# A recurrence and an MLP in float32: the first MLP product as three one-pass products of 12-bit parts

## The chip, the cores and the metric

The kernel runs on one core of a Trainium2 chip. The metric is the device time of one execution in microseconds (us). A core has a matrix engine (PE, TensorE), three engines for elementwise work (DVE or VectorE, ACT or ScalarE, POOL or GpSimd), an engine that only issues transfers here (SP), and DMA queues. Each engine works through its own instructions in the order in which the program placed them, and waits for others by semaphores. PE writes its results to PSUM, a small memory in banks; DVE and ACT bring them from there to SBUF, the main working memory.

## The reference

Two blocks stand one behind the other. The first is a linear recurrence for each of 4 x 8 pairs of batch and head, with 768 steps of 48 channels:

```python
for t in range(S):
    cur = einsum('bhd,bhe->bhde', u[None] * k_t, v_t)
    y[:, :, t] = einsum('bhd,bhde->bhe', r_t, state + cur)
    state = w_t[:, :, :, None] * state + einsum('bhd,bhe->bhde', k_t, v_t)
```

Its output, with the heads side by side, is x of 4 x 768 x 384. The second is a normalization and an MLP with 1536 hidden columns:

```python
xn = (x - mu) / sqrt(var + 1e-6) * g_ln
out = x + maximum(xn @ w_ch1, 0.0) @ w_ch2
```

All of it is float32.

## The kernel before

There are 8 rounds, each half of a batch's steps (384) for all heads; a round has two units of four heads. In a round the recurrence is solved by six levels of doubling blocks. At each level PE makes block products of r and k (`quads`, tile `a_ps`), DVE multiplies r and k by decays (`grow`), and DVE copies the wanted blocks into A with a mask (`keep`):

```python
def grow(q, lev, which="rk"):          # one unit
    ...
    for nm in which:
        ...
        DVE.tensor_tensor(out=X, in0=X, in1=T[...].broadcast_to(blocks), op=ALU.mult)

def keep(rnd, lev):
    for j in range(2):
        ...
        DVE.copy_predicated(out=out_j[:, :, :, 1, :], mask=mask, data=ps_j)
```

After the levels, the next round's first levels carry the states (`states`: PE makes `kv`, DVE a chain of small multiply-adds `s`) and the outputs (`outputs`: PE makes `y`, DVE adds it to `vo`). Inputs come with time on the partitions and are turned by PE with an identity matrix, three 128x128 pieces into one PSUM tile that ACT copies out (`turned` for w, k and r, `ends` for `kn`, `turned_x` for the normalized x):

```python
ps_t = ctx.enter_context(tc.tile_pool(name="ps_t", bufs=2, space=PSUM))
ps_a = ctx.enter_context(tc.tile_pool(name="ps_a", bufs=2, space=PSUM))
ps_m = ctx.enter_context(tc.tile_pool(name="ps_m", bufs=2, space=PSUM))
```

The MLP of a round is a generator of 24 steps. Twelve steps make one h tile each, and twelve steps make three o products each (in round 0 two of the o tiles run together):

```python
def mlp(rnd):
    ...
    for f in range(FC):                # FC = 12
        converted(KC * (f * P // WC + 1))
        ps = ps_m.tile([P, RN], F32, tag="m", name=f"h_ps{name}_{f}")
        for kc in range(KC):           # KC = 3
            PE.matmul(ps, w1_sb[:, kc, ts(f, P)], xT[:, kc, :], start=kc == 0, stop=kc == KC - 1)
        hs.append(ph.tile([P, RN], F32, tag="h", name=f"h{name}_{f}"))
        ACT.activation(out=hs[f], in_=ps, func=AF.Relu)
        yield
    # then: for each of three row tiles, 12 products with w2_sb into o_ps,
    #       DVE adds x into a tile o, SP sends o out
```

The main loop goes through rounds and levels. Each slot of round and level issues `quads`, `grow` and `keep`, and then `fill(UNTIL[slot], tasks)` lays a list of other tasks (transposes, loads, copies) evenly between MLP steps until a given number of steps is done. A round's MLP starts late in the next round's levels; from round 3 on a slot holds four steps, so that the h tiles of one round's MLP fall into level 5 and levels 0 and 1, and its o products into levels 2 to 4. During rounds 0 and 1 the weights are also brought into a rounded form by ACT and DVE (`begin`, `join`). `warm` issues matmuls whose results nobody reads.

Of the kernel before, what the change touches and what calls it, by code (L numbers as in the profile page):

```python
# [9 lines left out]
F32 = mybir.dt.float32  # L10
F16 = mybir.dt.float16
I8 = mybir.dt.int8
# [5 lines left out]
PSUM = bass.MemoryType.PSUM  # L18

# [25 lines left out]
def kernel(  # L53
# [45 lines left out]
    p6 = ctx.enter_context(tc.tile_pool(name="p6", bufs=6))  # L99
    low = ctx.enter_context(tc.tile_pool(name="low", bufs=4))  # L100
    ph = ctx.enter_context(tc.tile_pool(name="ph", bufs=12))
    ps_t = ctx.enter_context(tc.tile_pool(name="ps_t", bufs=2, space=PSUM))
    ps_a = ctx.enter_context(tc.tile_pool(name="ps_a", bufs=2, space=PSUM))
    ps_m = ctx.enter_context(tc.tile_pool(name="ps_m", bufs=2, space=PSUM))
# [8 lines left out]
        for nm in "wkr"  # L113
    }
    vn, vx, xs = {}, {}, {}
# [6 lines left out]
    def load(q, which="wkr", eng=SP):  # L122
        for nm in which:
            src = {"w": w, "k": k, "r": r}[nm]
            for j in range(NH):
                eng.dma_start(
                    out=nat[nm][q % 2][:, ts(j // 2, TT), j % 2, 0:D], in_=steps(src, q, j)
                )

    def load_v(q, eng=SP):  # L130
        vn[q] = p4.tile([P, NH, TT, D], F32, tag="v", name=f"v{q}")
        for j in range(NH):
            eng.dma_start(out=vn[q][:, j], in_=steps(v, q, j))

    def load_vx(q, eng=SP):

        vx[q] = p4.tile([P, NP, TT, D], F32, tag="vx", name=f"vx{q}")
        for i in range(2):
            eng.dma_start(
                out=vx[q][ds(C * (1 - i), C)].rearrange("p r c d -> p r (c d)"),  # L140
                in_=vn[q][ds(C * i, C)]
                .rearrange("p (r j) c d -> p r j (c d)", j=2)[:, :, 1],
            )
# [25 lines left out]
    for nm in "wkr":  # L169
        for t in nat[nm]:  # L170
            POOL.memset(t[:, :, :, D:HP], 0.0)
# [8 lines left out]
    for lev in range(NLEV - 1):  # L180
# [21 lines left out]
    w1_sb = const.tile([P, KC, DF], F32, name="w1_sb")  # L202
# [3 lines left out]
        (w1_sb[:, kc, ds(c, WC)], moe_w_ch1[ts(kc, P), ds(c, WC)])  # L206
# [59 lines left out]

    def warm(n):

        ps = ps_m.tile([P, RN], F32, tag="m", name="idle")
        for _ in range(n):  # L270
            PE.matmul(ps[:, 0:P], zeros, zeros, start=True, stop=True)


    st, carry = {}, {}

    def turned(q, nm, pr):
        a = st.setdefault(q, {})
        if pr == 0:
            if nm == "w":
                if q % U == 0:  # L280
                    st["w"] = p1.tile([P, U, W], F32, tag="w", name=f"wT{q // U}")
                a["w"] = st["w"][:, q % U]
            else:
                a[nm] = p4.tile([P, W], F32, tag=nm, name=f"{nm}T{q}")
        ps = ps_t.tile([P, RN], F32, tag="t", name=f"{nm}_ps{q}_{pr}")
        for c in range(TT):
            PE.transpose(
                ps[:, ts(c, P)],
                nat[nm][q % 2][:, pr * TT + c].rearrange("p j d -> p (j d)"), ident,
            )  # L290
        ACT.copy(out=a[nm][:, ts(pr, RN)], in_=ps)

    def totals(rnd, eng):

        tot = p1.tile([P, U, W], F32, tag="tot", name=f"tot{rnd}")
        T = [st["w"]]
        at, n = 0, W // 2
        for lev in range(NLEV):
            pair = T[lev].rearrange("p u (q two) -> p u q two", two=2)
            if lev < NLEV - 1:  # L300
                t = tot[:, :, at : at + n]
            else:
                t = p3.tile([P, U, NM], F32, tag="decay", name=f"decay{rnd}")
            eng.tensor_tensor(out=t, in0=pair[..., 0], in1=pair[..., 1], op=ALU.mult)
            T.append(t)
            at, n = at + n, n // 2
        for q in units_of(rnd):
            st[q]["T"] = [t[:, q % U] for t in T]


    def own_products(q, eng):
        b, f, g = units[q]
        rk = st[q]["rk"] = p1.tile([P, NK, 2, D], F32, tag="rk", name=f"rk{q}")
        eng.tensor_tensor(
            out=rk, in0=nat["k"][q % 2][:, :, :, 0:D], in1=nat["r"][q % 2][:, :, :, 0:D],
            op=ALU.mult,
        )
        by_tile = rk.rearrange("p (r c) j d -> p r c (j d)", r=NP)
        eng.tensor_tensor(
            out=by_tile, in0=by_tile,  # L320
            in1=u_bc[:, ts(g, NH)].rearrange("p (r j) d -> p r (j d)", j=2)[:, :, None]
            .broadcast_to([P, NP, TT, 2 * D]), op=ALU.mult,
        )
# [9 lines left out]
    def own_by_pe(q):  # L333
        b, f, g = units[q]
        a = st[q]
        ps = ps_t.tile([P, RN], F32, tag="t", name=f"own_ps{q}")
# [16 lines left out]
    def own_term(q, eng):  # L353
        a = st[q]
        a["vo"] = p4.tile([P, NH, TT, D], F32, tag="vo", name=f"vo{q}")
        eng.tensor_tensor(
            out=a["vo"], in0=vn[q],
            in1=a["own"][:, :, :, None].broadcast_to([P, NH, TT, D]), op=ALU.mult,
        )
# [23 lines left out]
    def grow(q, lev, which="rk"):  # L383

        n = 1 << lev
        a = st[q]
        T = (a["T"][lev] if lev else a["w"]).rearrange("p (q two) -> p q two", two=2)
        blocks = [P, W // (2 * n), n]
        for nm in which:
            i = "kr".index(nm)  # L390
            X = a[nm].rearrange("p (q two n) -> p q two n", two=2, n=n)[:, :, i, :]
            DVE.tensor_tensor(
                out=X, in0=X, in1=T[:, :, 1 - i][:, :, None].broadcast_to(blocks), op=ALU.mult
            )
# [3 lines left out]
    def keep(rnd, lev):  # L398
        n = 1 << lev
        A, ps = a_bufs[rnd % 2], a_ps[rnd]  # L400
        for j in range(2):
# [6 lines left out]
            else:  # L408
                mask = masks[lev][:, None].broadcast_to([P, U * NK, C // (2 * n), n])
                DVE.copy_predicated(out=out_j[:, :, :, 1, :], mask=mask, data=ps_j)  # L410
# [15 lines left out]
    def ends(q, pr):  # L426

        a = st[q]
        if pr == 0:
            a["kn"] = p2.tile([P, NK, P], F32, tag="kn", name=f"kn{q}")  # L430
        ps = ps_t.tile([P, TT, P], F32, tag="t", name=f"kn_ps{q}_{pr}")
# [4 lines left out]
    def states(q):  # L436
# [3 lines left out]
        s = a["s"] = p4.tile([P, NP, 2 * TT, D], F32, tag="s", name=f"s{q}")  # L440
        before = carry.get((b, g))
        kv = ps_a.tile([P, 2, 512], F32, tag="a", name=f"kv{q}")
# [9 lines left out]
        for m in range(2 * TT - (f == NHALF - 1)):  # L452
            for pr in range(NP):
                new = kv[:, m % 2, pr * TT + m // 2, :]
                if m == 0 and before is None:
                    DVE.tensor_copy(out=s[:, pr, m, :], in_=new)
                else:
                    c = pr * 2 * TT + m
                    DVE.scalar_tensor_tensor(
                        out=s[:, pr, m, :], in0=s[:, pr, m - 1, :] if m else before[:, pr, 2 * TT - 1, :],  # L460
# [3 lines left out]
        carry[b, g] = s  # L464
# [11 lines left out]
    def outputs(q):  # L476
# [7 lines left out]
        for k_ in range(NK):  # L484
# [9 lines left out]
            for i in range(2):  # L494
                for j in range(2):
# [5 lines left out]
                    elif a["before"] is not None:  # L501
                        R, s = a["r"][rows, ts(2 * k_, C)], a["before"][rows, pr, 2 * TT - 1]
# [44 lines left out]
    def turned_x(rnd, kc):  # L547
        if kc == 0:
            xTs[rnd] = p1.tile([P, KC, RN], F32, tag="xT", name=f"xT{rnd}")
        ps = ps_t.tile([P, RN], F32, tag="t", name=f"xT_ps{rnd}_{kc}")  # L550
        for i in range(TT):
# [3 lines left out]
        ACT.activation(  # L555
            out=xTs[rnd][:, kc, :], in_=ps, func=AF.Copy, scale=g_sb[:, kc : kc + 1]
        )

    def mlp(rnd):
# [3 lines left out]
        for f in range(FC):  # L563
            converted(KC * (f * P // WC + 1))
            ps = ps_m.tile([P, RN], F32, tag="m", name=f"h_ps{name}_{f}")
            for kc in range(KC):
                PE.matmul(
                    ps, w1_sb[:, kc, ts(f, P)], xT[:, kc, :], start=kc == 0, stop=kc == KC - 1
# [3 lines left out]
            yield  # L572

        groups = ((0, 1), (2,)) if rnd == 0 else ((0,), (1,), (2,))
        at = 0
        for group in groups:
# [13 lines left out]
            for i in group:  # L590
                o = p2.tile([P, H, D], F32, tag="o", name=f"o{name}_{i}")
                DVE.tensor_tensor(out=o, in0=ps[i], in1=x[:, i], op=ALU.add)
                SP.dma_start(
                    out=out[b, ds(f0 * RN + i * P, P), :].rearrange("t (h d) -> t h d", d=D),
                    in_=o,
# [58 lines left out]
    grow(u0, 0)  # L654
# [10 lines left out]
    grow(u1, 0)  # L665
# [3 lines left out]
    for lev in range(1, NLEV):  # L669
# [9 lines left out]
        for which in ("rk",) if lev < NLEV - 1 else "kr":  # L679
            for q in (u0, u1):  # L680
                grow(q, lev, which)
# [31 lines left out]
    mlps.append(mlp(0))  # L713

# [8 lines left out]
    for rnd in range(1, NR + 1):  # L723
# [3 lines left out]
        for lev in range(NLEV):  # L727
# [11 lines left out]
            for which in ("rk",) if lev < NLEV - 1 else "kr":  # L739
                for q in now:  # L740
                    grow(q, lev, which)
            if now:
                if rnd <= 2 and lev == 0:
                    totals(rnd, DVE)
                keep(rnd, lev)
            tasks = []
            if rnd == 1:
                if lev < 2:
                    tasks += each(load, new, "kr"[lev], [SPO])
# [14 lines left out]
            if rnd == 2 and lev == 0:  # L764
                tasks += each(load_v, now) + each(load, new, "w")
            if rnd == 2 and lev == 2:
                for q in now:
                    take(DVE, q)
                    tasks += each(load, new[q % U :][:1], "kr")
            if rnd == 2 and lev in (3, 4):  # L770
                tasks += each(own_term, now[lev - 3 :][:1], [POOL])
            if rnd > 2 and lev < 2:
                tasks += each(load, new, ["w", "kr"][lev])
# [13 lines left out]
            if lev == 3 and rnd > 1:  # L787
                for q in now:
                    load_vx(q)
                for q in new:  # L790
                    load_v(q)
# [6 lines left out]
            if lev == 5:  # L798
                if rnd > 2 and new:
                    own_sums(new[0])  # L800
                if rnd == 2:
                    tasks += each(own_products, new[:1], [POOL]) + each(own_sums, new[:1])
                if rnd >= 2:
                    tasks += each(own_term, new[:1], [POOL])
# [4 lines left out]
                if rnd >= 2:  # L809
                    tasks += each(own_sums, new[1:]) + each(own_term, new[1:], [POOL])  # L810
# [37 lines left out]
```

## Time and profile before

| | before |
|---|---|
| time, median of 3 runs | 620.29 us (620.15 to 621.03) |
| span of the profiled execution | 624.0 us |
| PE busy | 588.7 us, 8588 matmul records |
| DVE, ACT, POOL busy | 294.2, 199.2, 70.2 us |
| DMA moved | 36.83 MB |
| matmul groups `o_ps`, `h_ps`, `a_ps` | 205.5, 198.4, 82.1 us |

Busy time counts an interval once where instructions of an engine overlap; a mean duration counts each instruction with its overlap. Matmuls are pipelined, so that the spacing of their starts, and not their duration, is their rate. "PEld" are the loads of PE's stationary operand. In a group's row, the part after the last bar is the idle time of the engine just before these instructions, with what ended it. The chain is the sequence of work and waits that leads back from the last instruction to the first. Tile names carry the program's names without numbers; all instructions of the kernel have one line, that of the helper which keeps program order.

### The profile page before, as it was taken

To read this page: it belongs to the slowest core of one execution; us is meant where nothing else is said; L and a number is where in the kernel's file an instruction comes from. 1 tells how busy PE (TensorE), PEld (TensorE's weight loads), DVE (VectorE), ACT (ScalarE), POOL (GpSimd) and SP (SyncE) were. 2 spreads that over 40 slices of the span, in tenths; PEclk is the share of its full clock that TensorE was granted. 3 is DMA by queue.
4 is the path that set the end of the run, shared out by engine and by line. 5 is a ranking of instruction groups with operands and counts; after the bars stand their busy time and mean duration, and the time that the engine had idled before them with its cause. 6 is when DMAs were issued, how large, how long until landed. Compare 5 with 4: busy or idle time off the path is not lost.

```text
span 624.0 us, 19313 instructions
## 1 busy us (share of the span) xinstructions
PE 588.7 (94%) x8588; PEld 401.3 (64%) x8588; DVE 294.2 (47%) x706; ACT 199.2 (32%) x430; POOL 70.2 (11%) x100
## 2 busy tenths in 40 slices
PE   8969887987999999999999999999999999999997
PEld 7859554555666676667666676676666766566554
DVE  3854986785544755444437253553336352130000
ACT  3535675540135321431143212531142105301200
POOL 5000000000216100700051002500050000000000
PEclk9786898986699999999999999998999999999999
DMA  7872788103343241223220430211000000000000
GB/s 113 186 174 67 176 212 209 47 3 84 65 85 59 39 95 44 40 41 76 48 52 12 78 75 15 39 22 43 23 15 2 15 15 15 0 15 25 1 13 26
DMA packets 114962, 36.83 MB, mean 59 GB/s; under 512 B 104512, under 2 KB 111808, under 8 KB 114880
## 3 DMA queue, kind: packets, MB, share of 16 engines
q1 hardware_dynamic: 112464, 35.31, 25.2%
q8 instruction: 67, 1.10, 0.8%
q10 hardware_dynamic: 2416, 0.30, 0.4%
q14 instruction: 15, 0.12, 0.1%
HBM read 28.51 MB, written 4.72 MB: 53 GB/s over the span
## 4 chain that ended last, share of the span: by engine, by line
PE 80%; DVE 8%; SPq 4%; ACT 3%; DMA 2%; issue 2%; ACTq 0%; DVEq 0%
PE o_ps L49 30%; PE h_ps L49 28%; PE a_ps L49 10%; SPq L49 4%; PE y L49 3%; DVE w_sb L49 3%; PE kv L49 2%; PE r_ps L49 2%; DMA raw<-in_moe_w_ch_dram 1%; PE kn_ps L49 1%; PE k_ps L49 1%; PE xT_ps L49 1%; PE w_ps L49 1%; ACT rest L49 1%; DVE A L49 1%
## 5 line engine op out<-in xcount | busy, mean ns | idle before, releaser
L49 PE MATMUL o_ps<-w_sb,h 128*128 128x384 f32 x576 | 205.5, 504 | 2.5 <-DVE o L49 2.5
L49 PE MATMUL h_ps<-xT,w_sb 128*128 128x384 f32 x576 | 198.4, 494 | 0.6 <-DVE w_sb L49 0.6
L49 PEld LDWEIGHTS o_ps<-w_sb,h 128*128 128x128 f32 x576 | 108.5, 197 | 68.3 <-issue 5.9
L49 PEld LDWEIGHTS h_ps<-xT,w_sb 128*128 128x128 f32 x576 | 106.8, 192 | 66.9 <-DVE w_sb L49 1.9
L49 PEld LDWEIGHTS a_ps<-rT,kT 48*64 48x64 f32 x4608 | 77.0, 140 | 19.3 <-issue 16.3
L49 PE MATMUL a_ps<-rT,kT 48*64 48x32 f32 x4608 | 82.1, 224 | 6.2 <-issue 4.3
L49 ACT ACTIVATE h<-h_ps 128x384 f32<-128x384 f32 x96 | 46.5, 488 | 125.9 <-PE h_ps L49 125.7
L49 DVE TENSOR_TENSOR o<-o_ps,x 128x384 f32<-128x384 f32 x24 | 13.3, 556 | 132.4 <-PE o_ps L49 132.4
L49 POOL TENSOR_TENSOR vo<-v,own 128x576 f32<-128x576 f32 x12 | 14.3, 1194 | 390.8 <-DVE own L49 219.4
L49 DVE TENSOR_TENSOR rT<-rT,tot 128x384 f32<-128x384 f32 x80 | 44.5, 565 | 27.4 <-PE a_ps L49 27.4
L49 DVE COPY_PREDICATED A<-mask,a_ps 128x384 f32<-128x384 int8 x80 | 54.4, 748 | 0.0
L49 DVE TENSOR_TENSOR kT<-kT,tot 128x384 f32<-128x384 f32 x80 | 45.2, 566 | 9.2 <-PE a_ps L49 8.5
L49 DVE SCALAR_TENSOR_TENSOR s<-s,decay,kv 128x48 f32<-128x48 f32 x160 | 29.3, 258 | 28.1 <-PE kv L49 28.1
L49 DVE TENSOR_TENSOR x<-y,vo 128x288 f32<-128x288 f32 x32 | 13.1, 452 | 51.5 <-PE y L49 51.4
L49 ACT ACTIVATE xT<-xT_ps,g_sb 128x384 f32<-128x384 f32 x24 | 13.7, 580 | 70.5 <-PE xT_ps L49 70.4
L49 ACT COPY kT<-k_ps 128x384 f32<-128x384 f32 x32 | 14.6, 480 | 39.9 <-PE k_ps L49 39.9
L49 ACT COPY rT<-r_ps 128x384 f32<-128x384 f32 x32 | 14.4, 480 | 39.6 <-PE r_ps L49 39.5
L49 PEld LDWEIGHTS y<-v,A 64*64 64x64 f32 x384 | 20.8, 133 | 7.3 <-issue 6.0
L49 PE MATMUL kn_ps<-ident,kT 128*128 128x128 f32 x96 | 15.4, 289 | 9.0 <-ACT kn L49 7.2
L49 PE MATMUL y<-vx,A 64*64 64x48 f32 x384 | 23.8, 222 | 0.0
L49 PE MATMUL y<-v,A 64*64 64x48 f32 x384 | 23.8, 222 | 0.0
L49 ACT COPY kn<-kn_ps 128x384 f32<-128x384 f32 x32 | 14.4, 479 | 29.1 <-PE kn_ps L49 29.1
(70 smaller groups left out, 568.4 us busy)
## 6 DMA issues: line engine op xcount, KB each, us to landing
raw<-in_moe_w_ch_dram SPq DMA_DIRECT2D x24, 384.0 KB, 4.7
nat_w<-in_w_dram SPq DMA_DIRECT2D x64, 72.0 KB, 2.5
nat_k<-in_k_dram SPq DMA_DIRECT2D x64, 72.0 KB, 2.4
v<-in_v_dram SPq DMA_DIRECT2D x64, 72.0 KB, 3.1
out_dram<-o SPq DMA_DIRECT2D x24, 192.0 KB, 1.9
nat_r<-in_r_dram SPq DMA_DIRECT2D x60, 72.0 KB, 2.4
vx<-v SPq DMA_DIRECT2D x32, 72.0 KB, 2.4
nat_r<-in_r_dram ACTq DMA_DIRECT2D x4, 72.0 KB, 3.5
```

The costliest lines, as they stand in the source:

```text
L49: return lambda *args, **kw: self.tc.keep_in_program_order(f(*args, **kw))
```

## The change

For rounds 1 to 7 the float32 products of w1 with x are replaced. Both operands are split into a high part H of 12 bits and a scaled rest L, so that `w = wH + wL/4096` and the like, each part exact in the float32r format, in which PE takes an operand in one pass. Three sums of products then give the result in the manner of Karatsuba: one of the differences of the parts, one of the low parts, one of the high parts; the last two share a PSUM tile. The difference of the weights' parts is written to DRAM once and streamed back for each round, two h tiles at a time, as it does not fit into SBUF. Round 0 and the second product stay as they were. DVE and ACT join the sums; the relu of a tile is issued one tile later.

```diff
+        for f in range(FC if rnd else 0):
+            g, cols = f // G, ts(f % G, P)
+            at = (rnd - 1) * FC + f
+            d = streamed[at // 2][:, at % 2]
+            xH, xL, xD = xT
+            hs.append(ph.tile([P, RN], F32, tag="h", name=f"h{name}_{f}"))
+            ps = ps_m.tile([P, RN], F32, tag="m", name=f"hd_ps{name}_{f}")
+            for kc in range(KC):
+                PE.matmul(ps, d[:, kc], xD[kc], start=kc == 0, stop=kc == KC - 1)
+            ACT.copy(out=hs[f], in_=ps)
+            ps = ps_m.tile([P, RN], F32, tag="m", name=f"h_ps{name}_{f}")
+            for kc in range(KC):
+                PE.matmul(ps, w1_l[g][:, kc, cols], xL[kc], start=kc == 0, stop=False)
+            for kc in range(KC):
+                PE.matmul(ps, w1_h[g][:, kc, cols], xH[kc], start=False, stop=kc == KC - 1)
+            DVE.scalar_tensor_tensor(
+                out=hs[f], in0=ps, scalar=1.0 + E12, in1=hs[f], op0=ALU.mult, op1=ALU.add
+            )
+            if f:
+                ACT.activation(out=hs[f - 1], in_=hs[f - 1], func=AF.Relu)
+            if f % 2:
+                stream(at // 2 + 3)
+            yield
```

The weights are split in twelve pieces (`halve`) during rounds 1 and 2, and x in `turned_x`:

```diff
+    def halve():
+        ...
+        ACT.activation(out=H, in_=whole, func=AF.Copy, scale=TOP)
+        POOL.tensor_tensor(out=rest_, in0=whole, in1=H.bitcast(F32), op=ALU.subtract)
+        ACT.activation(out=L, in_=rest_, func=AF.Copy, scale=1 / E12)
+        POOL.tensor_tensor(out=d, in0=H.bitcast(F32), in1=L.bitcast(F32), op=ALU.subtract)
+        SPO.dma_start(out=w1_d[...], in_=d...)
...
+        ACT.activation(out=H, in_=xf, func=AF.Copy, scale=TOP)
+        DVE.tensor_tensor(out=L, in0=xf, in1=H.bitcast(F32), op=ALU.subtract)
+        DVE.scalar_tensor_tensor(out=nd, in0=H.bitcast(F32), scalar=-E12, in1=L.bitcast(F32), ...)
```

From round 1 on `grow` and `keep` act on both units at once, so that a level has one operation of 768 elements where it had two of 384. They are also no longer issued ahead of a slot's tasks but stand first in the task list, so that MLP steps may fall between them:

```diff
-            for which in ("rk",) if lev < NLEV - 1 else "kr":
-                for q in now:
-                    grow(q, lev, which)
+            tasks = []
             if now:
                 if rnd <= 2 and lev == 0:
                     totals(rnd, DVE)
-                keep(rnd, lev)
-            tasks = []
+                tasks += each(grow, [now], [lev], "rk" if lev < NLEV - 1 else "kr")
+                tasks += each(keep, [rnd], [lev])
```

Memory is rearranged to make room. In PSUM the transposes have one buffer and the MLP three; only before the main loop do transposes also take turns in the MLP's buffers (`spread`). In SBUF v, its exchanged copy, `vo` and the states have two buffers where they had four, r shares the input buffer of w and is loaded a level later, `kn` overwrites k, and the output is summed in place in x:

```diff
-    ps_t = ctx.enter_context(tc.tile_pool(name="ps_t", bufs=2, space=PSUM))
+    ps_t = ctx.enter_context(tc.tile_pool(name="ps_t", bufs=1, space=PSUM))
     ps_a = ctx.enter_context(tc.tile_pool(name="ps_a", bufs=2, space=PSUM))
-    ps_m = ctx.enter_context(tc.tile_pool(name="ps_m", bufs=2, space=PSUM))
+    ps_m = ctx.enter_context(tc.tile_pool(name="ps_m", bufs=3, space=PSUM))
...
-        vn[q] = p4.tile([P, NH, TT, D], F32, tag="v", name=f"v{q}")
+        vn[q] = p2.tile([P, NH, TT, D], F32, tag="v", name=f"v{q}")
...
-            a["kn"] = p2.tile([P, NK, P], F32, tag="kn", name=f"kn{q}")
+            a["kn"] = a["k"].rearrange("p (k n) -> p k n", n=P)
...
-                o = p2.tile([P, H, D], F32, tag="o", name=f"o{name}_{i}")
-                DVE.tensor_tensor(out=o, in0=ps[i], in1=x[:, i], op=ALU.add)
+                DVE.tensor_tensor(out=x[:, i], in0=ps[i], in1=x[:, i], op=ALU.add)
```

## The prediction

> **What bounds the kernel now.** I read the page first: the busy shares, the 40 slices with the granted clock, and the split of the chain that ended last.
>
> ```profile
> PE 588.7 (94%) x8588; PEld 401.3 (64%) x8588; DVE 294.2 (47%) x706; ACT 199.2 (32%) x430; POOL 70.2 (11%) x100
> PE   8969887987999999999999999999999999999997
> PEclk9786898986699999999999999998999999999999
> PE 80%; DVE 8%; SPq 4%; ACT 3%; DMA 2%; issue 2%; ACTq 0%; DVEq 0%
> ```
>
> TensorE is busy nearly always and carries 80% of the chain. Slices are 15.6 us wide; after the thirteenth (200 us) PE and its clock both show 9. A table by stage makes that exact (columns: the stretch, its length, then busy us and count of PE, weight loads, DVE, ACT, POOL; then clock, DMA share, GB/s).
>
> ```profile
> 0.00:131.00 131.00, 108.28 (x1889) 83.76 (x1889) 89.47 (x217) 74.15 (x158) 9.14 (x38) 0.88 0.62 141
> 131.00:200.00 69.00, 64.36 (x995) 43.21 (x999) 37.33 (x76) 16.41 (x38) 13.16 (x10) 0.83 0.33 66
> 200.00:574.00 374.00, 369.73 (x5574) 247.34 (x5568) 165.23 (x412) 102.73 (x223) 47.92 (x52) 1.00 0.16 35
> 574.00:624.00 50.00, 46.32 (x144) 26.98 (x142) 2.15 (x4) 5.88 (x12) 0.00 (x0) 0.99 0.04 16
> ```
>
> From 200 us PE idles about 4 of 374 us at full clock, DVE works 44% and ACT 27%. Here each us saved on PE is a us, as long as no new wait takes its place. Before 200 us start-up, weight conversion and a lower clock count too. Next, the two MLP groups (name and shapes, count | busy, mean ns | idle before), and the chain's end (start, length, what):
>
> ```profile
> L49 PE MATMUL h_ps<-xT,w_sb 128*128 128x384 f32 x576 | 198.4, 494 | 0.6 <-DVE w_sb L49 0.6
> L49 ACT ACTIVATE h<-h_ps 128x384 f32<-128x384 f32 x96 | 46.5, 488 | 125.9 <-PE h_ps L49 125.7
> ...
> 573.88 23.22 PE h_ps L49 x72
> 597.10 23.23 PE o_ps L49 x72
> ```
>
> 288 products appear as 576 records, two for each f32 product. The mean of 494 ns contains overlap; the rate is in the last line pair: 72 records in 23.22 us, 322.5 ns each, **645 ns a product, 1.935 us for an h tile** of three. Today DVE has no part in emptying h.
>
> **What the Trainium skill says.** "FP8 and Floating Point Precision", section TensorE Precision Notes: true FP32 takes four passes, reduced-precision FP32 reads are truncated to FP22. "TensorE: Matmul & The Clock Gate", section Back-to-back issue gap, gives N/2.4 + 2.5 ns for a pass, 162.5 ns at N = 384. The trace agrees: 645/4 = 161 ns. So I take 161 ns for a one-pass product, an estimate, as no float32r product is in this trace. The same page, section LDWEIGHTS, estimates 107 ns for 128 columns; the f32 pairs here load in 190 ns, latency included, and start with the preceding matmul. The `own_ps` pairs, with only two moving columns, follow each other every 213 ns at about half clock, so a load should hide behind 161 ns. "SBUF — State Buffer", section SBUF: two separate sides, calls the port pair of VectorE and GpSimd an exclusive lock. The trace agrees: while GpSimd multiplies, one DVE product takes three times as long as its twin just after.
>
> ```profile
> 396.46 1.40 POOL L49 TENSOR_TENSOR rk<-nat_k,nat_r 128x576 f32<-128x576 f32 x1
> 397.94 1.60 POOL L49 TENSOR_TENSOR rk<-rk,u_bc 128x576 f32<-128x576 f32 x1
> ...
> 398.20 1.76 DVE L49 TENSOR_TENSOR kT<-kT,wT 128x384 f32<-128x384 f32 x1
> 399.88 0.55 DVE L49 TENSOR_TENSOR rT<-rT,wT 128x384 f32<-128x384 f32 x1
> ```
>
> **The change, part by part.**
>
> *Products.* Rounds 1 to 7 have 84 h tiles. Each becomes 9 one-pass products: 9 x 161 = 1.45 us in place of 1.935, so 0.48 x 84 = **40 us less** on PE. Round 0 and all o products stay f32.
>
> *Emptying h.* Each tile now takes an ACT copy of the difference sum (PSUM, 0.48 us like `kn<-kn_ps`), a DVE multiply-add out of PSUM (0.56 like `o<-o_ps,x`) and an ACT relu (some 0.5). That adds 84 x 0.56 = 47 us of DVE and about 41 of ACT; the parts of x add 42 DVE and 21 ACT operations, 23 and 10 us. DVE goes to some 0.6 of the span, ACT to 0.43. By throughput neither binds.
>
> *Merged levels.* Two 384-wide operations start 0.47 us apart and end in 0.55; one of 768 is 0.87 + 0.08 (the 768-wide `tot` took 0.95). A pair thus saves only some 0.07 us of DVE. The masked copies cost 1.0 in levels 0 and 1 and 0.56 later. All of it saves perhaps 10 us of DVE that lay off the path; I count 2 us.
>
> *PSUM.* Transposes have one buffer instead of two after the prologue. Where two sets of three transposes (0.33 us each) stand next to each other in PE's order, the second waits for the copy: 0.1 from PE's issue to ACT's start, 0.48, 0.06 back, **0.64 us**. In the changed order I count seven such places a round: two among `kn`, two among `w`, one each among `k`, `r` and `xT`. The kernel before loses some 0.5 a round. Five rounds with all seven: 5 x (7 x 0.64 - 0.5) = 20; round 7 with three: 1.4. **About 21 us more.**
>
> *Queue order.* Steady h tiles lie in level 5 and levels 0 and 1 of the next round, where DVE and ACT also do the recurrence. I walked one such stretch with these durations.
> Level 5: ACT has four A copies (0.48 each) behind the last `kn` copy, ahead of the copy of the third difference sum; the fourth tile waits for its buffer some 1.0 us.
> Level 0: state updates (10 x 0.175 us apart), two grows (0.87 each), then the add of tile 4. Delayed by level 5, this frees the buffer about 1.0 us late for tile 6.
> Level 1, from kv's start: kv ends at 0.84, a_ps at 2.23, tiles 8 and 9 at 5.13, first `w` set at 5.46. DVE runs states to 2.69, grows to 4.43, masked copy to 6.0 and the add of tile 8 to 6.6; its relu ends at 7.15; only then may ACT copy `w`, to 7.6. The next `w` set starts at 7.7 and not at 6.1: 1.6 more.
> Together 3.6 us for each of four rounds and about 2 for round 7: **about 16 us**.
>
> *Round 1 and 2.* Twelve splittings of w1: 24 ACT operations (12 us) and 24 on GpSimd of some 0.83 (20 us), mostly beside PE; the first streamed difference must be written and read again. I put +2. Streaming moves 42 x 393 KB = 16.5 MB; a weight fetch of this size landed in 3.0 us at best and 4.7 in the median, against 2.9 us of products per pair of tiles. In the last round, which has only products, perhaps 1 us shows.
>
> Sum: 620.3 - 40 - 2 + 21 + 16 + 2 + 1 = 618. The walk takes each arrival at its latest and adds delays that may overlap (a late PE lets DVE catch up), so I shade this to **614 us**.
>
> **Rivals.**
> (a) The waits overlap and PE stays the bound with idle time as today. For it: DVE and ACT have free time, and round 6's and 7's products, some 24 tiles, meet little recurrence. That gives about 585 to 600.
> (b) DVE and ACT queues become the bound in the h stretch, a wait taking the place of the saved passes, and PE's lower use lowers its clock, as in the first 200 us (0.83 to 0.88 there with PE busy 83 to 93%). 625 to 640.
> (c) The one-pass pair is bound by its weight load, not by 161 ns. If 190 ns were the interval, a tile would take 1.71 us and the saving would be 19 us: about 635. Against it: the 190 contains latency, as the own_ps spacing suggests.
> (d) Late streamed weights hold PE. DMA is at 0.16 busy after 200 us, against it; one issuing queue in order, in which value exchanges wait for their own loads, speaks for it. Up to 10 us.
>
> **Range and chances.** The gain of 40 is the surest number; the losses of 37 could be half or a third more: 620 - 42 + 20 = 598, 620 - 42 + 50 = 628, widened for start-up and clock to 596 to 635. The 2% bounds are 608 and 633. Faster by over 2% 0.35, within 0.54, slower 0.11.
>
> **What would show it.** One-pass records of h spaced 161 ns. Total PE time down by some 40 us while its idle time after 200 us goes from 4 to 30 us or more. Waits of PE's transposes for ACT copies near 20 us in sum, and h matmuls waiting for DVE. Granted clock still 1.0. DVE near 0.6. The last 36 products of h taking 17.5 to 18.5 us instead of 23.2. I am wrong if PE's idle time stays under 15 us (then below 600), if records are spaced 190 ns, or if the clock falls.

## The result and the profile after

| | before | after |
|---|---|---|
| time, median | 620.37 us (620.15 to 621.03) | 690.15 us (687.5 to 692.29) |
| ratio, 95% interval | | 1.113 (1.1099 to 1.1162) |
| span of the profiled execution | 624.0 us | 689.1 us |

The change costs 70 us. That is outside the predicted range of 596 to 635. The page of the kernel after, with the same lines that were shown of before: busy shares, the slices of PE and of its clock (now 17.2 us wide), the split of the chain.

```profile
PE 585.2 (85%) x8840; PEld 448.0 (65%) x8840; DVE 367.6 (53%) x708; ACT 262.7 (38%) x559; POOL 101.5 (15%) x124
PE   8988883948817889888998979988998999899997
PEclk9777877869958999999999999999999989999999
PE 61%; DVE 16%; ACT 12%; issue 4%; DMA 3%; SPq 3%; POOL 1%; ACTq 0%; POOLq 0%; DVEq 0%
```

PE's part of the chain fell from 80% to 61%; DVE's doubled to 16% and ACT's went from 3% to 12%. The seventh slice shows PE at 3, the ninth at 4, the twelfth at 1: holes of this depth are not in the kernel before, and they lie in rounds 1 and 2, where the prediction allowed 2 us. The table by stage (columns as before), with the stages cut at the first `kv` of rounds 2 and 3 and at the last round's products:

```profile
0.00:155.00 155.00, 119.48 (x1817) 89.58 (x1820) 94.71 (x184) 79.31 (x169) 22.20 (x50) 0.78 0.50 117
155.00:239.00 84.00, 58.38 (x1050) 46.20 (x1045) 51.37 (x82) 27.41 (x59) 25.52 (x21) 0.86 0.34 83
239.00:640.00 401.00, 362.51 (x5812) 278.65 (x5813) 211.39 (x424) 143.97 (x307) 53.74 (x54) 0.98 0.29 71
640.00:689.10 49.10, 44.82 (x188) 33.55 (x186) 10.18 (x19) 12.05 (x26) 0.00 (x0) 1.00 0.15 48
```

Second and third columns: in round 2 PE idles 25.6 of 84 us. From 239 to 640 us it idles 38.5 of 401, where before it idled 4.3 of 374. Now what PE waited for (waiter, releaser, us in total, times, longest):

```profile
PE kn_ps L45 <- ACT kT L45: 16.9, 15, 6.6
PE r_ps L45 <- ACT rT L45: 15.5, 10, 10.3
PE hd_ps L45 <- DMA w1d<-w1d: 14.3, 1, 14.3
PE w_ps L45 <- ACT wT L45: 12.7, 13, 2.1
PE k_ps L45 <- ACT kT L45: 10.9, 13, 2.3
```

Two kinds stand here. Four lines are transposes that wait for the copy out of their single PSUM buffer, mostly some 0.7 us at a time, with one wait of 10.3 and one of 6.6 among them. One line is a single wait of 14.3 us for the first streamed weights.

For all later comparisons, here is the length of each round, from its first state product `kv` to that of the next (us, one trace for each kernel):

| | prologue | round 1 | 2 | 3 | 4 | 5 | 6 | 7 | last stretch |
|---|---|---|---|---|---|---|---|---|---|
| before | 52.8 | 74.7 | 71.4 | 58.3 | 67.8 | 68.9 | 71.1 | 63.4 | 95.4 |
| after | 48.8 | 105.9 | 84.2 | 65.7 | 75.7 | 76.3 | 75.0 | 66.7 | 90.9 |
| f32_only | 50.8 | 87.9 | 65.6 | 65.1 | 74.0 | 75.4 | 75.2 | 69.1 | 95.3 |
| f32_only_2t | 45.6 | 76.0 | 67.0 | 59.2 | 68.5 | 69.6 | 69.8 | 67.3 | 95.6 |
| stream_first | 50.3 | 104.8 | 72.7 | 65.7 | 74.8 | 76.1 | 73.6 | 64.7 | 90.5 |
| late_split | 48.0 | 87.0 | 65.4 | 78.6 | 78.8 | 75.6 | 80.3 | 61.6 | 90.5 |
| two_t | 46.8 | 91.6 | 76.6 | 63.9 | 74.9 | 72.9 | 71.5 | 65.2 | 98.9 |
| one_sum | 50.5 | 106.2 | 80.9 | 62.6 | 71.7 | 70.4 | 70.2 | 64.8 | 88.9 |
| staged | 46.6 | 83.0 | 69.6 | 56.9 | 66.2 | 69.3 | 64.6 | 63.3 | 90.5 |
| staged_late | 47.6 | 75.8 | 67.0 | 59.5 | 68.6 | 64.6 | 70.2 | 59.6 | 89.6 |

Runs more than 1.5% above the fastest of their kernel, in a slower state, are left out of all times here, some of before and these: two of four of late_split, and three of twenty of one_sum_2t, whose profiled run is one of them, so that it has no row.

Rounds 1 and 2 grew by 31.2 and 12.8 us, rounds 3 to 7 together by 29.9. Only the prologue and the last stretch became shorter, the latter by 4.5. Round 1 in before, after, f32_only and f32_only_2t, with the columns of the table by stage:

```profile
52.80:127.50 74.70, 63.70 (x1022) 43.42 (x1022) 58.63 (x151) 49.71 (x105) 0.00 (x0) 0.90 0.55 135
48.80:154.70 105.90, 75.64 (x1026) 49.49 (x1026) 67.23 (x137) 56.92 (x120) 12.44 (x12) 0.75 0.38 94
50.80:138.70 87.90, 71.09 (x1022) 46.19 (x1022) 58.69 (x137) 50.15 (x105) 0.00 (x0) 0.83 0.39 98
45.60:121.60 76.00, 63.77 (x1022) 44.13 (x1022) 57.20 (x133) 49.77 (x106) 0.00 (x0) 0.91 0.50 124
```

With the change PE idles 30.3 us there instead of 11.0, and nearly the same number of matmuls keeps it busy 11.9 us longer, at a granted clock of 0.75 instead of 0.90.

### The profile page after: what moved, and what is told of

The parts are those of the page before. It is cut to its first block, busy times and chain, and to the rows that moved or that the text cites. A ratio compares the mean times of both kernels' runs of the same rounds, so it can differ in the third digit from the quotient of the medians.

```text
span 689.1 us, 20085 instructions
## 1 busy us (share of the span) xinstructions
PE 585.2 (85%) x8840; PEld 448.0 (65%) x8840; DVE 367.6 (53%) x708; ACT 262.7 (38%) x559; POOL 101.5 (15%) x124
## 4 chain that ended last, share of the span: by engine, by line
PE 61%; DVE 16%; ACT 12%; issue 4%; DMA 3%; SPq 3%; POOL 1%; ACTq 0%; POOLq 0%; DVEq 0%
PE o_ps L45 25%; PE h_ps L45 10%; PE a_ps L45 7%; PE hd_ps L45 4%; PE y L45 3%; SPq L45 3%; DVE rT L45 3%; DVE kT L45 3%; ACT kT L45 2%; DVE A L45 2%; DVE s L45 2%; PE w_ps L45 2%; PE k_ps L45 2%; PE r_ps L45 2%; ACT h L45 2%
## 5 line engine op out<-in xcount | busy, mean ns | idle before, releaser
L45 PE MATMUL o_ps<-w_sb,h 128*128 128x384 f32 x576 | 203.5, 501 | 0.5 <-issue 0.5
L45 DVE SCALAR_TENSOR_TENSOR h<-h_ps,h 128x384 f32<-128x384 f32 x84 | 46.0, 558 | 109.3 <-PE h_ps L45 63.6
L45 PEld LDWEIGHTS a_ps<-rT,kT 48*64 48x64 f32 x4608 | 76.3, 139 | 20.5 <-issue 15.9
L45 PE MATMUL hd_ps<-xd,w1d 128*128 128x384 f32 x252 | 64.6, 365 | 15.1 <-DMA w1d<-w1d 14.3
L45 ACT COPY h<-hd_ps 128x384 f32<-128x384 f32 x84 | 40.0, 476 | 78.8 <-PE hd_ps L45 78.0
L45 PE MATMUL h_ps<-xhl,w1l 128*128 128x384 f32 x252 | 61.1, 352 | 6.5 <-ACT h L45 4.3
L45 DVE TENSOR_TENSOR rT<-rT,tot 128x768 f32<-128x768 f32 (+1 forms) x45 | 45.2, 1005 | 39.6 <-PE a_ps L45 33.9
L45 PE MATMUL h_ps<-xhl,w1h 128*128 128x384 f32 x252 | 59.1, 343 | 0.0
L45 PEld LDWEIGHTS hd_ps<-xd,w1d 128*128 128x128 f32 x252 | 44.3, 195 | 16.8 <-issue 14.4
L45 DVE COPY_PREDICATED A<-mask,a_ps 128x768 f32<-128x768 int8 x40 | 53.4, 1334 | 0.0
L45 PEld LDWEIGHTS h_ps<-xhl,w1l 128*128 128x128 f32 x252 | 46.4, 195 | 10.0 <-ACT h L45 6.2
L45 DVE TENSOR_TENSOR kT<-kT,tot 128x768 f32<-128x768 f32 (+1 forms) x45 | 44.8, 995 | 4.3 <-PE a_ps L45 4.2
L45 PEld LDWEIGHTS h_ps<-xhl,w1h 128*128 128x128 f32 x252 | 46.9, 195 | 0.0
L45 POOL TENSOR_TENSOR rk<-nat_k,nat_w 128x576 f32<-128x576 f32 x10 | 15.6, 1560 | 210.4 <-DVE own L45 62.5
L45 ACT COPY rT<-r_ps 128x384 f32<-128x384 f32 x32 | 15.3, 478 | 54.2 <-PE r_ps L45 54.0
L45 POOL TENSOR_TENSOR w1rest<-w,w1h 128x384 f32<-128x384 f32 x12 | 13.5, 1122 | 138.7 <-DVE w_sb L45 96.4
```

Of the source, the lines that this page charges most:

```text
L45: return lambda *args, **kw: self.tc.keep_in_program_order(f(*args, **kw))
```

## The experiments

**f32_only.** The first product is f32 in all rounds; splitting, streaming and emptying through DVE are gone. Merged levels, memory and single transpose buffer stay.

```diff
-        for f in range(FC if rnd == 0 else 0):
+        for f in range(FC):
...
-        for f in range(FC if rnd else 0):
+        for f in range(0):
...
-                    tasks += [halve, halve]
...
```

> The changed kernel with the first product in f32 in all rounds: no splitting of w1 or x, no streamed differences, no adds; the merged levels, the one transpose buffer and the SBUF layout stay. Theory A (the time was lost to splitting in rounds 1 and 2, about 40 us, and in steady rounds to waits for the one transpose buffer and to queue order): rounds 1 and 2 return to near their old length, steady rounds lose 7 x 0.73 - 0.5 = 4.6 us each over five rounds; 640 to 650 us. Rival B (the rearrangement itself, levels issued among tasks and one transpose buffer, costs it all, in the first rounds too): the products' saving of 84 x 0.35 = 29 us is lost and nothing returns, 700 us or more.

Measured: 662.3 us, ratio 1.0704 (1.0665 to 1.0744). It fell between the two theories. So the one-pass scheme itself, its saved passes counted, accounts for 27.9 us of the loss (690.15 - 662.3) and what is left for some 42. PE's waits in this run:

```profile
PE kn_ps L45 <- ACT kT L45: 14.6, 16, 5.7
PE r_ps L45 <- ACT rT L45: 9.4, 9, 4.7
PE w_ps L45 <- ACT wT L45: 9.3, 13, 2.1
PE k_ps L45 <- ACT kT L45: 9.2, 13, 2.1
```

The same four names lead, without any one-pass product in the kernel.

**f32_only_2t.** As f32_only, with two transpose buffers and two for the MLP, as before.

```diff
-    ps_t = ctx.enter_context(tc.tile_pool(name="ps_t", bufs=1, space=PSUM))
+    ps_t = ctx.enter_context(tc.tile_pool(name="ps_t", bufs=2, space=PSUM))
...
-    ps_m = ctx.enter_context(tc.tile_pool(name="ps_m", bufs=3, space=PSUM))
+    ps_m = ctx.enter_context(tc.tile_pool(name="ps_m", bufs=2, space=PSUM))
```

> As f32_only, and the PSUM buffers as before: two for transposes, two for the MLP. What is left of the change is merged levels, their place in the task list and the SBUF layout. Theory A: within 1% of the kernel before, 618 to 628 us, and the difference to f32_only, some 20 us, is the price of the single transpose buffer. Rival B: if the late levels or the shared SBUF buffers cost, it stays above 640 us.

Measured: 620.02 us, ratio 1.0027 (1.0003 to 1.0051), as theory A had it. Merged levels, tasks placed later and the rearranged SBUF thus cost and gain nothing to speak of in sum, and **the exchange of a transpose buffer for a third MLP buffer costs 42.3 us** (662.3 - 620.0), twice the 20 expected. The waits of this run:

```profile
PE r_ps L45 <- ACT rT L45: 5.0, 3, 4.4
PE w_ps L45 <- ACT wT L45: 2.8, 4, 1.8
...
PE k_ps L45 <- ACT kT L45: 2.3, 3, 1.8
...
PE kn_ps L45 <- ACT kT L45: 1.8, 6, 0.4
```

The four lines sum to 11.9 us where they summed to 42.5. By the table, the difference is 5.2 us in the prologue, 11.9 in round 1, 22.6 in rounds 3 to 6 (5.4 to 5.9 each) and 1.8 in round 7; round 2 and the last stretch are 1.4 and 0.3 shorter. The prologue's part is not shown to be the buffer's: a wait of 5.7 us for one copy of `kn` stands there in f32_only, but with two buffers before has one of 5.5, and with one buffer after has 1.5.

**stream_first.** The first two streamed weight fetches are issued ahead of the loads of v, w and k in round 2, level 2.

```diff
             if rnd == 2 and lev == 2:
+                tasks += each(stream, [2])
+            if rnd == 2 and lev == 2:
                 tasks += each(load_v, now, [SPO])
...
-                tasks += each(stream, [2])
```

> The changed kernel with one move: the first two fetches of streamed differences are issued ahead of the 24 loads of round 2, level 2, not behind them. Theory A: the wait of 14.5 us before the first one-pass product goes, as it was the in-order issue queue (0.49 us a load); 690 - 14 = 676 us. Rival: the differences were not yet written anyway, or another wait ends just after; then 685 us or more.

The reason for it is in the timeline of SP, which only issues transfers, in the kernel after (start, length, what, count):

```profile
189.18 3.29 SPq L45 DMA_DIRECT2D nat_w<-in_w_dram  x4
192.52 2.07 SPq L45 DMA_DIRECT2D nat_k<-in_k_dram  x4
195.01 2.26 SPq L45 DMA_DIRECT2D nat_w<-in_w_dram  x4
197.32 2.08 SPq L45 DMA_DIRECT2D nat_k<-in_k_dram  x4
199.44 1.00 SPq L45 DMA_DIRECT2D w1d<-w1d  x2
```

An issue takes some 0.5 us, and the fetch stands behind these 16 loads of w and k and 8 of v, the first of them issued at 184.89; issued at 199.44, it releases PE at 203.5, after 14.3 us of waiting. Measured: 675.47 us, ratio 1.0936 (1.0876 to 1.0996): **14.7 us less**, by the table 11.5 in round 2 and 1.1 in round 1. As expected: the DMA engines were not the limit, the order of issue was.

**late_split.** Round 1's product stays f32 too, and the splitting moves from rounds 1 and 2 to round 3, three pieces a level in levels 1 to 4.

```diff
-        if rnd == 0:
+        if rnd < 2:
...
-                if lev >= 3:
-                    tasks += [halve, halve]
...
-            if rnd == 2 and lev < 3:
-                tasks += [halve, halve]
+            if rnd == 3 and 0 < lev < 5:
+                tasks += [halve, halve, halve]
```

> The changed kernel with round 1's first product in f32 too, and the twelve splittings of w1 moved from rounds 1 and 2 to round 3, levels 1 to 4, where ACT and GpSimd have room and no weight conversion shares the buffers. Theory A: rounds 1 and 2 get back 30 to 40 us, the f32 round costs 12 x 0.35 = 4 us, the splitting in round 3 a few; 655 to 665 us. Rival: splitting costs as much wherever it stands; 680 us or more.

Measured: 665.6 us, ratio 1.0756 (1.0701 to 1.0812), just above the 655 to 665 expected. Rounds 1 and 2 are back at 87.0 and 65.4, the values of f32_only, so their whole excess came from the splitting and what goes with it (the first fetch, round 1's one-pass products). But round 3 takes 78.6 us instead of the 65.1 of f32_only: some 13 us, with PE at a clock of 0.96, and its transposes waiting 14.1 us for ACT's copies there instead of 4.8. The weight conversion of the start is not needed for such a loss (though three pieces a level are denser than two). What the splitting does is seen in the chain of waits of the kernel after in round 1 (start, length, what):

```profile
107.57 0.57 DVE w_sb L45
...
108.31 1.00 POOL w1rest L45
...
109.33 0.53 ACT w1l L45
...
111.03 1.11 POOL w1rest L45
...
113.97 0.64 ACT rest L45
...
117.67 0.63 ACT rest L45
118.30 0.33 ACT rT L45
...
118.68 0.47 PE r_ps L45
```

`w1l` on ACT needs GpSimd's `w1rest`, and ACT runs in order: everything behind it, the weight conversions `rest` and at last the copy `rT` that frees the transpose buffer, waits with it. The first `w1rest` itself stood still, 5.1 us after its operand was there, until DVE had freed one of the four small buffers that it shares with the weight conversion (107.57); ACT stood 6.15 us in all before 109.33. PE gets to `r_ps` at 118.68, after its wait of 10.3 us; in f32_only, with the same conversions and no splitting, the longest is 4.7.

**two_t.** The kernel after with two transpose buffers and, in exchange, two for the MLP; the edit is that of f32_only_2t.

> The changed kernel, one-pass products and all, with PSUM as before the change: two buffers for transposes, two for the MLP (three in the changed kernel). Theory A (the single transpose buffer costs the 42 us by which f32_only stood over f32_only_2t, whatever the products): 650 us, less a loss, as the second sum of a tile now has to wait for the add of the tile before: an add takes 0.72 us from PE to PE, the difference sum in between 0.53, so 0.2 x 84 = 17 us and more where DVE is busy; 655 to 670. Rival: the third MLP buffer is worth as much as the second transpose buffer; 685 us or more.

Measured: 670.55 us, ratio 1.0842 (1.0752 to 1.0933), at the upper edge of what was expected: 20 us gained, not 42. A new line leads PE's waits:

```profile
PE h_ps L45 <- DVE h L45: 13.6, 33, 1.5
```

An h tile of the change takes two PSUM tiles, each held until ACT or DVE has emptied it; with two buffers the products wait 33 times for the add, and the last stretch, with few transposes to gain from, is 8.0 us longer. Either pool is short as long as there are two tiles for each h tile.

**one_sum.** All nine products of an h tile go to one PSUM tile; ACT's relu, with the scale, is the only operation behind it. The copy and DVE's multiply-add are gone. (The difference sum, too, is scaled by 1 + 1/4096.)

```diff
-            ACT.copy(out=hs[f], in_=ps)
-            ps = ps_m.tile([P, RN], F32, tag="m", name=f"h_ps{name}_{f}")
...
-            DVE.scalar_tensor_tensor(
-                out=hs[f], in0=ps, scalar=1.0 + E12, in1=hs[f], op0=ALU.mult, op1=ALU.add
-            )
-            if f:
-                ACT.activation(out=hs[f - 1], in_=hs[f - 1], func=AF.Relu)
+            ACT.activation(out=hs[f], in_=ps, func=AF.Relu, scale=1.0 + E12)
```

> The changed kernel with all nine products of a tile in one PSUM tile and one relu with scale 1 + 1/4096 out of it: no ACT copy, no DVE add, no second relu pass; the factor then also falls on the small difference sum, a change of relative size near 6e-8. PSUM buffers as in the changed kernel. Theory A (in steady rounds the saved passes were lost to h tiles waiting for DVE and ACT in queue order): steady rounds fall from 75.5 to 70 to 71 us, 690 - 25 = 665. Rival C (the passes never brought anything, as one-pass records come every 175 ns and the rest is lost to transposes): no more than 5 us better, 685 us.

Measured: 666.88 us, ratio 1.0811 (1.0726 to 1.0896), close to the 665 of theory A. **Emptying h through two tiles, ACT and DVE thus cost 23.3 us**, of which 21.7 lie from round 3 on. The edit takes away the copy, the add and the second tile at once, and the runs do not tell them apart. A stretch of the chain in the kernel after shows what went away:

```profile
318.96 1.25 DVE A L45
...
320.64 0.60 DVE h L45
...
321.26 0.02 ACT h L45
...
321.69 0.47 ACT wT L45
...
322.20 0.56 PE w_ps L45 x3
```

This is level 1 as the prediction walked it: the masked copy into A ends, only then comes the add of h, then a relu, then the copy of `w`, and only then may PE turn the next `w`.

**one_sum_2t.** one_sum with two buffers for each pool and the early fetches of stream_first.

> one_sum with two transpose buffers and two MLP buffers, and the first streamed differences fetched ahead of the loads as in stream_first. Theory A: f32_only_2t (620) - 84 x 0.35 (29) + splitting in rounds 1 and 2 (36.6 - 14.5 = 22) = 613 us; steady rounds of 65 us. Rival: with fewer passes some other wait (DVE levels, streamed weights) holds a round at 68 us; then 630 us or more.

Measured: 617.74 us, ratio 0.9997 (0.9972 to 1.0021). The three repairs bring 72 us and the kernel back to the time of before, 5 us short of what was expected.

**rates.** The kernel after, with 120 one-pass matmuls at its end whose results nobody reads: 24 for each of five shapes, with 64 or 128 weight columns and 256, 384 or 512 moving columns.

```diff
+    for cols, n in ((P, 384), (64, 384), (P, 256), (64, 256), (P, 512)):
+        ...
+        for _ in range(24):
+            PE.matmul(ps[0:cols, 0:n], w1_l[0][:, 0, 0:cols], src_[:, 0:n], start=True, stop=True)
```

> The changed kernel followed by 5 x 24 one-pass matmuls whose results nobody reads, for their spacing: weights of 128 or 64 columns, 384, 256 or 512 moving columns. If a weight load bounds the pair (rival c of the prediction, in a milder form): 175 ns for 128 columns at both 384 and 256 moving, about 216 at 512, and 161 at 384 with 64 columns. If the 14 ns belong to the pass itself: 122 ns at 256, and no change with 64 columns. The time is that of the changed kernel and some 25 us.

Timeline of PE in this run (start, length, what):

```profile
686.04 14.62 PE L45 MATMUL rate<-xhl,w1l 128*128 128x384 f32 x96
700.49 5.61 PE L45 MATMUL rate<-w1l,w1l 128*128 128x512 f32 x24
```

The starts of the single records give the median spacing: 177 and 176 ns for 384 columns with 128 and 64 weight columns, 118 ns for 256 with both, 227 ns for 512. Half the weight columns change nothing, and with 128 of them a matmul can follow every 118 ns, so no weight load sets the 177. As expected if the excess belongs to the pass itself: it is 11 to 17 ns above N/2.4, the granted clock being 1.0 there. The one run took 708.71 us.

**staged.** one_sum_2t, with each splitting cut in two: a first task does ACT's high part and GpSimd's rest, a second one, at the slot's end, does ACT's scaling and what follows. The rest stays in the low part's own tile, so that no small buffer has to come free.

```diff
-        POOL.tensor_tensor(out=rest_, in0=whole, in1=H.bitcast(F32), op=ALU.subtract)
-        ACT.activation(out=L, in_=rest_, func=AF.Copy, scale=1 / E12)
...
+        POOL.tensor_tensor(out=L, in0=whole, in1=H.bitcast(F32), op=ALU.subtract)
...
+    def halve2():
...
+        ACT.activation(out=L, in_=L.bitcast(F32), func=AF.Copy, scale=1 / E12)
+        ...
```

> one_sum_2t with each splitting of w1 cut in two: the high part and the rest at the front of a slot's tasks, the scaling, the difference and its write at the end of the slot, and the rest kept in the low part's own tile. ACT then never stands waiting for GpSimd in front of the transposes' copies, and two of four conversion buffers are free again. Theory A (the 16 us that round 1 lost against f32_only_2t are ACT's queue held up by the splitting): round 1 falls from 92 to 78 to 82 us; 603 to 608 us. Rival: it is the work itself (24 ACT and 24 GpSimd operations beside the weight conversion); no change, 615 to 618 us.

Measured: 608.26 us, ratio 0.9879 (0.9807 to 0.995). Waits of PE:

```profile
PE r_ps L45 <- ACT rT L45: 6.1, 3, 5.5
```

The longest wait for `rT`, 10.0 us in two_t with the same transpose buffers, is 5.5 here, near the 4.4 of f32_only_2t, which has no splitting. Round 1 takes 83.0 us; with two buffers and unstaged splitting it took 91.6 (two_t), without splitting 76.0 (f32_only_2t). The stages thus recover 8.6 of 15.6 us, nearly all of it idle time of PE (24.7 us in two_t, 16.7 here): more than half of the loss there was ACT's queue held up, and not the work as such. Two things changed at once, though, the issue in two stages and the need for a small buffer, and they are not told apart. Time and round 1 are just above what was expected (608 and 82).

**staged_late.** As staged, with round 1's product f32, and the splitting spread two pieces a slot over the last two levels of round 2 and the first four of round 3.

```diff
-                if lev >= 3:
-                    tasks += [halve, halve]
+            if 10 <= slot < 16:
+                tasks += [halve, halve]
...
+            if 10 <= slot < 16:
+                tasks += [halve2, halve2]
```

> As staged, and round 1's first product stays f32, so that the splitting can stand in six slots of rounds 2 and 3, two pieces a slot, after the weight conversion has ended. Theory A: rounds 1 and 2 as in f32_only_2t (76 and 67), rounds 2 to 3 some us longer for the splitting, then 65 us a round; 620 - 72 x 0.35 (25) + 3 = 597 to 602 us. Rival: the splitting costs its 15 to 18 us there too, as it did in late_split (78.6 against 65.1); 612 us or more.

Measured: **603.03 us, ratio 0.9764 (0.9679 to 0.9849)** against before in the same comparison (618.12 us), a us above what was expected. It is faster than both kernels; whether by 2% of before, the interval leaves open. Its page (busy, clock), and its stage from the first `kv` of round 3 to the start of the last stretch:

```profile
PE 562.7 (93%) x8804; PEld 433.2 (72%) x8804; DVE 315.8 (52%) x618; ACT 217.8 (36%) x472; POOL 102.7 (17%) x124
...
PEclk9786899979999999998999999998999999999999
```

```profile
190.00:512.90 322.90, 311.81 (x5373) 244.89 (x5371) 177.13 (x321) 108.61 (x237) 76.67 (x74) 0.99 0.36 86
```

PE idles 11.1 of 322.9 us; rounds 1 and 2 take 75.8 and 67.0, as in f32_only_2t, and round 3 takes 59.5 (59.2 in f32_only_2t) with three quarters of the splitting in it, 18 of the 24 operations on each of ACT and GpSimd.

## Why the prediction was wrong

The mechanisms of the large terms were named; two terms were sized far too small, and those two alone are 56 of the missing 76 us.

*What bounds the kernel: right.* PE is still the bound where nothing waits: the last stretch, which is mostly MLP, became 4.5 us shorter, and staged_late gains as soon as PE's waits are gone.

*Products, -40: too large.* The step that failed is "I take 161 ns for a one-pass product". The formula of the Trainium skill, "TensorE: Matmul & The Clock Gate", section Back-to-back issue gap, gives an estimate of 162.5 ns for this shape; the section calls it the gap of an isolated matmul and says that in a stream the weight loads count too, which the prediction passed over. The runs show 176 ns on average in the kernel after and 177 in rates, where no weight load sets it, and the measurement decides. A tile of nine takes 1.585 us and not 1.45, as the chain of the last round shows:

```profile
644.04 0.53 PE hd_ps L45 x3
644.57 1.06 PE h_ps L45 x6
645.63 0.53 PE hd_ps L45 x3
646.16 1.06 PE h_ps L45 x6
```

The saving is 0.35 x 84 = 29 us. The last round's 12 tiles took 19.9 us with a wait of 0.7 among them, not 17.5 to 18.5.

*Merged levels, -2: right in that nothing came of them.* f32_only_2t is at 1.0027 of before. The runs don't separate them from the other rearrangements there.

*Single transpose buffer, +21: measured 42.* The mechanism is the one predicted; a set that stands behind another waits for ACT's copy, in the chain 298.3 to 300.5 us of the kernel after:

```profile
298.75 0.56 PE kn_ps L45 x3
299.31 0.02 issue
299.34 0.49 ACT kT L45
299.82 0.04 issue
299.87 0.56 PE kn_ps L45 x3
```

Wait and copy alternate, and each adjacent set loses 0.73 to 0.83 us instead of 0.64. Rounds 3 to 6 lose 22.6 us by it and round 7 1.8, a little over the predicted 21. The term failed because it counted only steady rounds. In round 1, 11.9 us longer with one buffer, PE idles 4.6 us more: ACT's queue also holds weight conversions there, so that copies come up to several us after the transposes. The other 7.3 us are the same 1022 matmul records keeping PE busy longer (71.1 against 63.8), at a clock of 0.83 against 0.91; why the clock was lower, no run shows. The 5.2 us of the prologue stay open.

*Queue order, +16: measured 23.* That emptying costs in this way is shown by one_sum; the size was short. The waits of h's own products for ACT and DVE are 7.3 us in sum in the kernel after, and those of `w` and `k` for their copies are 6.5 us shorter in one_sum; the split of the rest is not shown.

*Splitting in rounds 1 and 2, +2: measured +36.6.* This is the step that failed worst. After less f32_only is 105.9 - 87.9 in round 1 and 84.2 - 65.6 in round 2. Some 13 of it is the order of issue on SP (stream_first): rival (d) in its mechanism, which put at most 10 us on it. For the other 24 us the words that failed are "mostly beside PE": they add up busy time and leave out that an ACT operation in the middle of a chain ACT, POOL, ACT, POOL blocks the queue for the copies that PE needs. Issuing that chain in stages recovers 8.6 of the 15.6 us that it costs round 1 with two buffers. Two more things show in the traces, and how much of them reached PE is not told apart. One fits the lock between VectorE and GpSimd that the prediction itself quotes and did not count here: DVE's 36 conversion operations `w_sb` of round 1 take 15.3 us in f32_only, 22.3 in the kernel after, beside GpSimd's splitting, and 17.3 in staged. The other is the clock: of the 18.0 us by which round 1 grew from f32_only to the kernel after, PE's idle time makes 13.5, and 4.6 are nearly the same matmuls keeping it busy longer, at 0.75 instead of 0.83.

*Streaming at the tail, +1: nothing.* In the last round PE waits for no streamed weights; its one wait of 0.7 us between tiles is for DVE's add of h (655.26 to 655.83).

*Balance.* 620 + 42 (transpose buffer) + 37 (rounds 1 and 2) - 2 (prologue) - 4 (from round 3 on) is 693, against 690 measured. The -4 is the sum of after less f32_only over rounds 3 to 7 and the last stretch: the gain of the passes, less the 23 us of emptying. So of the 40 us that the scheme was to bring, 4 were left there.

*The rivals.* (a) did not occur. (b) came nearest in kind: DVE and ACT took the place of PE in the chain, though busy only 53% and 38%. Its rule for the clock does not follow from its figures, as PE busy 83% had the clock of 0.88 there and PE busy 93% that of 0.83; after the change, PE busy 90% had 0.98 from 239 to 640 us. (c), the pair bound by its weight load, is refuted by rates. Of the signs named, PE's idle time after 200 us came true (38.5 us from 239 us on); DVE nearly (0.53); the clock in the steady rounds (0.98), but not in round 1 (0.75). PE's busy time was to fall by 40 us and fell by 3.5 (by 26.0 in staged_late, where PE hardly waits). The spacing of 161 and "waits near 20 in sum" did not come true either: the four lines of transposes' waits for ACT copies shown above sum to 56.0.

## What to carry to other kernels

Before operations are added to an engine that is mostly idle, follow its queue and not its busy share: an operation that waits in the middle of it holds every copy behind it, and so PE. Cut chains across two engines into stages issued far enough apart, and issue the fetch that PE needs first ahead of loads that have time. A PSUM buffer that is taken away costs a full round trip at each place where two users stand together (0.73 to 0.83 us here), and more where the emptying engine's queue is crowded; so fewer PSUM tiles for each result (one sum for nine products) brought as much here (23 us) as one more buffer (20).

## What the runs showed of the hardware

One-pass float32r matmuls follow each other every 118, 177 and 227 ns for 256, 384 and 512 moving columns, 11 to 17 ns above N/2.4, with 64 weight columns as with 128 (at 256 and 384; within 1 ns); the two records of an f32 product with 384 moving columns lie 322.5 ns apart, only 2.5 ns above 2 x 160. An h tile of nine one-pass products thus costs 1.585 us against 1.935 for three f32 products, 0.82 of it and not three quarters. Why a one-pass matmul has the larger gap stays open. An issue on SP took some 0.5 us, so that 24 loads in front of one fetch held it up for 14.5 us (184.89 to 199.44), with the DMA engines a third busy. DVE's 384-wide `w_sb` operations took 0.36 us each in f32_only and up to 1.15 us in the kernel after; the 7 of 24 that took longer than 0.42 us all overlapped GpSimd's splitting.
